# A fused attention and max-out kernel on one core: another head, column tiles for some output products, and a new order of the list

## The chip, the cores and the metric

The kernel runs on one core of a Trainium2 chip. The core has TensorE (matrix products; the profile shows its matmuls as PE and its weight loads as PEld), VectorE (DVE), ScalarE (ACT), GpSimd (POOL) and SyncE (SP), which run side by side and wait for one another by semaphores, and 16 DMA engines that serve queues issued here by SP and POOL. TensorE writes its results to PSUM, eight banks of 512 float32 columns in each of 128 partitions; DVE and ACT read them from there. The metric is the time of one execution on the device in microseconds, and its median over several runs. Less is better.

## The reference

Two attention steps through 32 inducing vectors, for each of four batches of 12544 rows of 128 channels, then a max-out layer over all 50176 rows:

```python
    scale = 1.0 / np.sqrt(C)
    I = np.broadcast_to(inducing[None], (B, m, C))

    def mab(q, kv):
        s = scale * (q @ kv.transpose(0, 2, 1))
        s = s - s.max(-1, keepdims=True)
        a = np.exp(s)
        a /= a.sum(-1, keepdims=True) + 1e-09
        return a @ kv
    h = mab(I, x)
    return mab(x, h).astype(np.float32)
...
    h1 = x @ w1
    h2 = x @ w2
    g = np.maximum(h1, h2)
    return (g @ w_out).astype(np.float32)
```

The sizes: x is 4 x 12544 x 128, inducing 32 x 128, w1 and w2 128 x 1024, w_out 1024 x 128, all float32.

## The kernel before

*What is computed.* The kernel first finds, for each batch, h (32 x 128), the pooled rows. It then never forms the second attention's output: it multiplies h by w2 - w1 ahead of time (`hwd`, 32 x 1024) and by w1 w_out (`m1`, 32 x 128), and uses max(a, b) = a + relu(b - a). For each chunk of 128 rows the exponentials of the scores against h (`e2`, 32 x 128) times `hwd` give the arguments of the ReLU (eight blocks of 128 x 128, laid with the hidden channel on the partitions); the ReLU's result times w_out is added up over the eight blocks in PSUM, and the product of `e2` and `m1`, called the linear part, is added to the same bank. At the end each row is scaled by the reciprocal of the sum of its 32 exponentials.

*The tiling.* A batch has 98 chunks. Four chunks, or runs of chunks, called quarters, form a block: the four quarters sit in the four groups of 32 partitions. TensorE is used in three modes. In full mode one product uses the whole array: the 3136 output products of line 932 (weights 128 x 128 from the ReLU's result, 128 columns of w_out), transposes, and the sums over the batch. In row mode the array is cut in four tiles of 32 rows, and four products of 512 columns run side by side, one for each quarter: `phase`, line 1085, both the ReLU's arguments (`e,hwd`) and the linear part (`m,e`). In column mode the array is cut in four tiles of 32 columns, again side by side: the scores of a block (`stage`, line 657), those of the pooling (`pool_scores`, line 356), and the pooling's sums (`pool_accum`, line 414).

*The stages.* The head (up to some 22 us) loads batch 0 in parts, transposes them on TensorE (`p1_transpose`, line 276; DVE copies one half of a part out of PSUM, ACT the other), takes their scores (line 292), exponentials (ACT, line 305), and adds up two sums in PSUM: line 319 (products with a column of ones, up to four chunks of 32 as weights) and line 328 (with x). All parts but the first are loaded by POOL's queue, which casts float32 to float16 on the way. w1 and w2 follow in halves, then w_out. Then come the sums' turn, the first 256 columns of `hwd`, the first block's scores (`stage_first`, line 684), and the main list. It works off the blocks of batch 0 and does the pooling of batch 1 between them, and so on; from batch 1 on x is transposed by DMA (line 208).

*What sets the order.* All engines but the DMAs run in the order in which the program is written. The main list is a string, `ORDER`, one word for each piece of work: a plain number is so many output products, `p4.13` a phase of four quarters (the second number's bits swap the engine chosen for a ReLU), `s` stages the next block, `x`, `c`, `t`, `a` are steps of the pooling, `g` turns the exponentials of a block for their sums (SP's transposing DMA, then POOL), `H`, `W` the late part of the weights (`H1` makes the second half of `hwd` and transposes the second half of w1; `W` multiplies w1 by w_out, line 607). `EVICT` says for each group of output products whether DVE or ACT scales it. While the program is built, the class `Clock` keeps an account of when each engine will be free; it decides which PSUM bank is taken (the one free first), whether ACT or DVE takes a ReLU (the one that would be done first), and whether filler products are put in (`keep_busy`, line 891). Nothing of it runs on the chip.

*Buffers.* Eight PSUM banks are eight tags of one pool; ReLU results have two buffers of 128 x 4096 float16 for each quarter; six output tiles wait for their stores, which SP issues.

## Time and profile before

| what | value |
|---|---|
| median of 3 runs | 318.21 us (317.64 to 318.43) |
| the profiled execution, its own time | 317.76 us |
| its span, first to last instruction | 316.0 us |
| granted clock of TensorE | 0.998 |
| TensorE's last product ends | 312.9 us after the span's start |
| busy shares: PE, ACT, DVE, POOL | 98%, 89%, 87%, 40% |
| HBM read and written | 27.28 MB, 25.69 MB |

The time of a run has about 1.8 us more in it than the span, which counts from the first instruction to the last. A busy share adds up the time in which at least one instruction of the engine is in flight; TensorE's products are pipelined (one of 128 columns is in flight for 219 ns, and the next starts after 56), so 98% doesn't say that nothing can be saved. Where an engine's idle time is given, the name behind the arrow is what ended it.

### The profile page before, as it was taken

The numbers are of one execution on the slowest core, as the hardware profiler recorded it, in microseconds if no ns is written. First come the engines' busy times: TensorE is split into PE (matmuls) and PEld (weight loads), VectorE is DVE, ScalarE is ACT, GpSimd is POOL, SyncE is SP. The second block draws the span as 40 slices with busy tenths as digits, with TensorE's granted clock in tenths as the row PEclk, the third lists the DMA queues.
The fourth block names the chain that finished last, engine by engine and source line by source line (L and its number), as shares of the span: only waits on it lengthen the run. The fifth ranks groups of instructions, "written<-read, shape, count | busy, mean of one in ns | idle before, by whom it ended". The sixth has DMA issues, their size and how long they took to land.

```text
span 316.0 us, 12577 instructions
## 1 busy us (share of the span) xinstructions
PE 308.6 (98%) x5308; PEld 239.9 (76%) x5308; DVE 274.5 (87%) x488; ACT 280.2 (89%) x580; POOL 125.8 (40%) x187
## 2 busy tenths in 40 slices
PE   6998999999999999999999999999999999999996
PEld 3885777777877777778877787887868777788885
DVE  2468999999878999988999899989899889999885
ACT  3669999999999999998999989899999999998891
POOL 7363060666620066067510064674406564461500
PEclk9999999999999999999999999999999999999999
DMA  8999999989799999898499999897323233324232
GB/s 203 208 252 205 207 219 146 207 229 230 127 218 245 245 183 174 190 233 207 121 225 252 213 227 215 204 174 203 106 85 118 100 106 118 119 88 140 102 120 101
DMA packets 81336, 55.81 MB, mean 177 GB/s; under 512 B 62816, under 2 KB 66176, under 8 KB 81280
## 3 DMA queue, kind: packets, MB, share of 16 engines
q1 hardware_dynamic: 75312, 41.32, 55.8%
q0 software_dynamic: 5968, 13.70, 22.4%
q8 instruction: 41, 0.67, 0.9%
q14 instruction: 15, 0.12, 0.1%
HBM read 27.28 MB, written 25.69 MB: 168 GB/s over the span
## 4 chain that ended last, share of the span: by engine, by line
PE 94%; DMA 2%; ACT 1%; DVE 1%; issue 1%; POOL 0%; POOLq 0%
PE ps L932 60%; PE ps L1085 23%; DMA xn<-in_x_dram 2%; PE ps L657 2%; PE ps L356 2%; PE ps L414 2%; PE ps L276 1%; PE ps L328 1%; PE ps L292 1%; PE ps L521 0%; DVE relu L1105 0%; PE ps L319 0%; ACT e L669 0%; DVE o L964 0%; ACT e_first L696 0%
## 5 line engine op out<-in xcount | busy, mean ns | idle before, releaser
L1102 ACT ACTIVATE relu<-ps 128x512 f16<-128x512 f32 x470 | 241.0, 627 | 17.5 <-PE ps L1085 16.5
L1105 DVE TENSOR_SCALAR relu<-ps 128x512 f16<-128x512 f32 x314 | 199.7, 684 | 20.6 <-PE ps L1085 19.0
L932 PE MATMUL ps<-woutp,relu 128*128 128x128 f16 x3136 | 203.5, 219 | 0.2
L932 PEld LDWEIGHTS <-relu 128*128 128x128 f16 x3136 | 176.6, 98 | 34.4 <-issue 28.7
L1085 PE MATMUL ps<-e,hwd 32*128 32x512 f16 (+2 forms) x840 | 82.8, 361 | 0.1
L720 POOL TENSOR_TENSOR half<-ed 128x256 f32<-128x256 f16 (+2 forms) x23 | 14.1, 613 | 145.8 <-DMA ed<-e 145.8
L724 POOL TENSOR_TENSOR rd<-den,minus 128x16 f32<-128x16 f32 (+2 forms) x23 | 60.7, 2639 | 1.8
L964 DVE TENSOR_TENSOR o<-ps,rd 128x512 f32<-128x512 f32 (+3 forms) x83 | 53.2, 643 | 3.9 <-PE ps L1085 2.8
L1085 PE MATMUL ps<-m,e 32*128 32x128 f16 x372 | 36.8, 216 | 0.0
L1085 PEld LDWEIGHTS <-hwd 32*128 32x128 f16 x880 | 26.7, 91 | 12.8 <-issue 3.8
L1085 PEld LDWEIGHTS <-e 32*128 32x128 f16 x372 | 22.4, 92 | 10.4 <-issue 2.7
L720 POOL TENSOR_TENSOR half<-half 128x32 f32<-128x32 f32 (+3 forms) x69 | 22.3, 323 | 5.4
L195 POOL DMA_DIRECT2D xn<-in_x_dram x32 | 17.6, 563 | 5.7 <-DMA xn<-in_x_dram 4.3
L280 DVE COPY xT<-ps 128x512 f16<-128x512 f16 (+3 forms) x12 | 5.7, 485 | 8.6 <-PE ps L276 8.6
L964 DVE TENSOR_TENSOR o<-ps,rp 128x512 f32<-128x512 f32 (+3 forms) x20 | 12.8, 642 | 0.0
L369 ACT ACTIVATE eu<-ps 128x512 f16<-128x512 f32 x18 | 11.0, 617 | 0.6 <-PE ps L356 0.3
L669 ACT ACTIVATE e<-ps 128x512 f16<-128x512 f32 (+2 forms) x21 | 11.1, 607 | 0.3 <-PE ps L657 0.2
L283 ACT COPY xT<-ps 128x768 f16<-128x768 f16 (+3 forms) x10 | 5.7, 574 | 4.3 <-PE ps L276 4.2
L276 PE MATMUL ps<-identity,xn 128*128 128x128 f16 x98 | 7.6, 220 | 1.4 <-DMA xn<-in_x_dram 0.9
L657 PE MATMUL ps<-xT,hT 128*32 128x512 f16 (+3 forms) x110 | 8.1, 361 | 0.1
L276 PEld LDWEIGHTS <-xn 128*128 128x128 f16 x98 | 5.5, 97 | 2.9 <-DMA xn<-in_x_dram 1.2
L356 PE MATMUL ps<-xT,inducingT 128*32 128x512 f16 x72 | 6.8, 386 | 0.0
(110 smaller groups left out, 117.7 us busy)
## 6 DMA issues: line engine op xcount, KB each, us to landing
out_dram<-o SPq DMA_DIRECT2D x90, 256.0 KB, 3.0
xn<-in_x_dram POOLq DMA_DIRECT2D x24, 448.0 KB, 10.4
out_dram<-o SPq DMA_DIRECT2D x10, 128.0 KB, 2.9
wf<-in_moe_w_dram POOLq DMA_DIRECT2D x4, 256.0 KB, 6.0
xn<-in_x_dram POOLq DMA_DIRECT2D x4, 224.0 KB, 10.2
xT<-xn SPq DMA_TRANSPOSE x33, 4.4
xf<-in_x_dram SPq DMA_DIRECT2D x1, 512.0 KB, 3.7
xf<-in_x_dram SPq DMA_DIRECT2D x1, 384.0 KB, 4.2
```

The lines of the kernel that those rows point to most:

```text
L195: nc.gpsimd.dma_start(out=xn_at[b, i][:, 0:n, :], in_=xr[b, :, k0 : k0 + n, :])
L276: nc.tensor.transpose(ps[:, j, :], xn[:, g + j, :], identity16)
L356: nc.tensor.matmul(out=ps[32 * g : 32 * (g + 1), :], lhsT=inducingT, rhs=xT_tiles[b % 2][:, U * u + 4 * g : U * u + 4 * (g + 1), :], start ...
L657: nc.tensor.matmul(out=ps[32 * q : 32 * (q + 1), 128 * t : 128 * (t + n)], lhsT=hq, rhs=xT[:, c : c + n, :], start=True, stop=True, tile_p ...
L669: nc.scalar.activation(out=blk.e2[:, 0 : 128 * wd], in_=ps[:, 0 : 128 * wd], func=AF.Exp, scale=st[0]["rs"] if blk.b == 0 else scale,)
L720: nc.gpsimd.tensor_tensor(out=dst, in0=cur[:, :, 0:n], in1=cur[:, :, n : 2 * n], op=ALU.add)
L724: nc.gpsimd.tensor_tensor(out=rp[:, 0:wd, :].rearrange("p t q -> p (t q)"), in0=den[:, 0 : 4 * wd], in1=minus1[:, 0 : 4 * wd], op=ALU.pow,)
L932: nc.tensor.matmul(out=g.ps[:, 128 * c : 128 * (c + 1)], lhsT=g.blk.relu[g.q][:, 128 * (jb * w4 + t) : 128 * (jb * w4 + t + 1)], rhs=woutp ...
L964: nc.vector.tensor_mul(osb[:, 0:m, :], g.ps[:, 0 : m * C].rearrange("p (s c) -> p s c", s=m), g.blk.rp[:, t0 : t0 + m, q : q + 1].broadcas ...
L1085: nc.tensor.matmul(**seq.pop(0))
L1102: nc.scalar.activation(out=dst, in_=src, func=AF.Relu)
L1105: nc.vector.tensor_scalar(out=dst, in0=src, scalar1=0.0, scalar2=None, op0=ALU.max)
```

## The change

The head: batch 0 is cut in 13 parts in place of 12 (the first from POOL's queue has 7 chunks). Parts 0 and 2 to 7 land as float32 in buffers that are free at that time (`homes`); DVE casts one half of a part, POOL the other (`cast_x`), and POOL's remaining loads are issued one by one between its casts (`load_next`), so each is behind the cast ahead of it. The sums with ones (line 319 before) take whole groups of four chunks: the exponentials stand in buffers padded with zeros, and the last two parts of two chunks are summed together. The order of the head's words is another, some copies out of PSUM change between DVE and ACT (`x` behind the word), and the sums over the identity go ahead of the first cast. The difference w2 - w1 is split in other pieces: DVE has one of 256 columns, POOL one of 256 and one of 512. POOL in place of ACT casts the second half of w1, before the last four loads of batch 1. The eight transposes of w1 go together, out of the head, into the list (`V`).

Output products in column tiles: a count with an `n` in the list puts each product as four, of 32 weight columns each, in the four column tiles. There are 44 such counts, 511 of the 3136 products, most of them beside `s`, `c` or `a`.

The list: all words of `ORDER`, the bits behind the phases, and `EVICT` are new. A third number of a phase holds ReLUs back: if the next unit of that quarter lands in the next bank, one instruction does both (1024 columns); `u` lets held ones go. 32 ReLUs become double. ACT evicts 38 pieces of 128 columns in place of 11.

The account (`Clock`): other constants, switching times by the mode that is left, a count of instructions fed to TensorE. Buffers: the eight banks are one tile, the ReLU buffers and output tiles are fixed in place of drawn from pools.

```diff
-    PAIR = 0.0558
-    SWITCH = {"full": 0.11, "row": 0.097, "col": 0.097}
+    PAIR = 0.0559
+    COLS = 0.0562
+    SWITCH = {
+        "full": {"row": 0.095, "col": 0.095},
+        "row": {"full": 0.082, "col": 0.088},
+        "col": {"full": 0.1, "row": 0.094},
+    }
+    STEP = 0.0035
+    FEED = 0.0133
+    AHEAD = 1.2
     LAT = 0.20
-    ROW = 0.224
...
-    def on_act(self, ready, us, tail=0.12):
+    def feed(self, n):
+        self.fed = max(self.fed, self.pe - self.AHEAD) + self.FEED * n
...
+    psall = psum.tile([128, 8, 512], F32, name="psall", tag="psall")
+    relus = [big.tile([128, 2, 4096], F16, name=f"relus{q}", tag=f"relus{q}") for q in range(4)]
+    relu1 = [big.tile([128, 1024], F16, name=f"relu1_{q}", tag=f"relu1_{q}") for q in range(2)]
...
-    parts[0] = [(0, 14), (14, 14), (28, 14), (42, 14), (56, 7), (63, 7), (70, 7), (77, 7), (84, 6), (90, 4), (94, 2), (96, 2)]
+    parts[0] = [(0, 14), (14, 7), (21, 7), (28, 14), (42, 14), (56, 7), (63, 7), (70, 7), (77, 7), (84, 6), (90, 4)]
+    parts[0] += [(94, 2), (96, 2)]
...
+        homes = {0: (2, 0, 0, 14), 2: (0, 1, 0, 7), 3: (1, 1, 0, 14), 4: (2, 1, 0, 14)}
+        homes.update({5: (0, 1, 7, 7), 6: (3, 1, 0, 7), 7: (3, 1, 7, 7)})
+        wide = {}
+        for i, (q, slot, k, n) in homes.items():
+            w = relus[q][:, slot, 256 * k : 256 * (k + n)].bitcast(F32)
+            wide[i] = w.rearrange("p (k c) -> p k c", c=C)
...
+        later = []
+        for i, (k0, n) in enumerate(parts[0]):
+            if i:
+                later.append((wide.get(i, xn_at[0, i]), xr[0, :, k0 : k0 + n, :]))
...
+        def load_next():
+            dst, src = later.pop(0)
+            nc.gpsimd.dma_start(out=dst, in_=src)
...
+        def cast_x(i):
+
+            for half, (g, m) in enumerate(cut(parts[0][i][1])):
+                eng = nc.gpsimd if half else nc.vector
+                eng.tensor_copy(out=xn_at[0, i][:, g : g + m, :], in_=wide[i][:, g : g + m, :])
+                done = ck.on_pool(LANDED[i], 0.1 + 0.19 * m) if half else ck.on_dve(LANDED[i], 0.05 + 0.083 * m)
+                st[0]["cast", i, half] = done
+            load_next()
...
+        pair16 = head16[:, 1024 : 1024 + 4 * M].rearrange("p (k m) -> p k m", m=M)
+        ets = {}
+        for ids, at, n in ((0, 3, 4), 1152, 14), ((1, 2, 5, 6), 2688, 7), ((9,), 3712, 6), ((10,), 3968, 4):
+            room = 4 * ((n + 3) // 4)
+            some = head16[:, at : at + len(ids) * room * M].rearrange("p (i k m) -> p i k m", i=len(ids), m=M)
+            if room > n:
+                nc.vector.memset(some[:, :, n:room, :], 0.0)
+            for j, i in enumerate(ids):
+                ets[i] = some[:, j]
...
+                if n > 2:
+                    cuts = [(et, j, 4) for j in range(0, n, 4)]
+                else:
+                    cuts = [(pair16, 0, 4)] if last else []
+                for src, j, m in cuts:
                     nc.tensor.matmul(
-                        out=st[0]["eps"][0 : m * M, 0:1],
-                        lhsT=et[:, j : j + m, :].rearrange("p k m -> p (k m)"),
...
-        1a 1b I S0 2a 2b S1 A0 S2 3a 3b A1 4a 4b S3 S4 A2 A3 5a 5b A4 6a 6b S5 7a 7b S6 A5 8a 8b S7
-        A6 9a 9b 10a S8 11a N S9 S10 A7 S11 A8 A9 A10 A11
+        1a 1b 0b C2 I 2b 2a S0 C3 S1 C4 S2 A0 A2 C5 3b A1 3ax 4a 4b S3 5b C6 5a 6a S4 C7 A3 S5 6b A4 L
+        7ax 7bx S6 A5 8bx 8a 9a 9b S7 A6 10bx 10a 11ax S9 12a N S8 S10 A7 S11 S12 A9 A8 A10 A11 A12
...
+        load_x(1, 0)
+        difference(nc.vector, 0, 256, 20.45, 0.34)
+        difference(nc.gpsimd, 256, 512, 20.45, 0.64)
+        load_x(1, 1)
+        load_x(1, 2)
+        difference(nc.gpsimd, 512, J, 22.35, 1.25)
+        cast_w1(1)
+        for i in range(3, 7):
             load_x(1, i)
...
+                nc.gpsimd.tensor_copy(out=w1h[:, sl], in_=w1f[:, sl])
+                w_of["cast"] = ck.on_pool(0.0, 0.8)
+
+        def weights_2():
+            turned = []
+            for g in range(2):
+                bi, ps = bank([128, 4, 128], F16)
+                for j in range(4):
+                    jb = 4 * g + j
+                    nc.tensor.transpose(ps[:, j, :], w1h[:, 128 * jb : 128 * (jb + 1)], identity16)
+                turned.append((bi, ps, ck.run(0.056 * 4, ready=max(ck.bank[bi], w_of["cast"] if g else 0.0), why="w")))
+                ck.bank[bi] = INF
+            for g, (bi, ps, end) in enumerate(turned):
+                if g == 0:
+                    nc.vector.tensor_copy(out=w1T[:, 0:4, :], in_=ps)
+                    ck.bank[bi] = w_of["w1T"] = ck.on_dve(end, 0.34)
+                else:
+                    nc.scalar.copy(out=w1T[:, 4:8, :], in_=ps)
...
+        def final_one(narrow=False):
...
+            tiles = [(32 * i, 32 * (i + 1)) for i in range(4)] if narrow else [(0, 128)]
+            for lo, hi in tiles:
+                nc.tensor.matmul(
+                    out=g.ps[lo:hi, 128 * c : 128 * (c + 1)],
+                    lhsT=relu[:, lo:hi],
+                    rhs=woutp[:, jb, :],
+                    start=not g.started,
+                    stop=(state["mm"] + 1 == n * NJB and g.linear),
+                    tile_position=(0, lo) if narrow else None,
+                    skip_group_check=True,
+                )
             g.started = True
-            end = ck.run(ck.PAIR)
+            ck.feed(8 if narrow else 2)
+            if narrow:
+                ck.wait(ck.fed, "feed")
...
+            on_act, on_dve = ((0.48, 0.6), (0.907, 1.133))[n - 1]
+            if (max(ck.act, ready) + on_act <= max(ck.dve, ready) + on_dve) != flip:
+                nc.scalar.activation(out=dst, in_=src, func=AF.Relu)
+                t = ck.on_act(ready, on_act)
+            else:
+                nc.vector.tensor_scalar(out=dst, in0=src, scalar1=0.0, scalar2=None, op0=ALU.max)
+                t = ck.on_dve(ready, on_dve)
+            for bi in banks:
...
+                near = [c for c, j in enumerate(free) if q in holds and c not in paired and j == holds[q][2] + 1]
+                if near:
+                    free[a], free[near[0]] = free[near[0]], free[a]
+                    paired.append(a)
...
+                if q in holds and k in paired:
+                    _, first, b0, _ = holds.pop(q)
+                    relu_out((q, blk), [first, unit], [b0, bi], ready, bool(flip >> k & 1))
+                elif q in holds:
+                    _, first, b0, ended = holds.pop(q)
+                    relu_out((q, blk), [first], [b0], ended, False)
+                    relu_out((q, blk), [unit], [bi], ready, bool(flip >> k & 1))
+                elif hold >> k & 1 and nxt and nxt[1:3] == unit[1:3] and nxt[3] == unit[3] + 1:
+                    holds[q] = (blk, unit, bi, ready)
+                    ck.bank[bi] = INF
+                else:
...
-        s p4.13 s H1 W g2 p4.1 p2 8 m0 4 p3 p2.1 10 p3 p2 13 p3.2 6 p4.5 22 p2 p4.8 17 x1.0 p4.8 4 g1 11
-        p4.1 13 p4.9 p1 16 p3.4 p2 14 p4.10 6 x1.1 4 x1.2 x1.3 x1.4 x1.5 x1.6 2 p3.6 s s s s 6 g3 6 p4.5
...
+        s p4.14.2 p1 s s s H1 V g2 4 p3.0.1 p2 W 2 p3.1 2 m0 9 p2.3.1 p3.1 x1.0 14 p2.2 p3 n17 x1.1 s
+        p4.9 x1.2 2 p2 n13 p4.3 n5 g3 n5 p4.6 11 g1 7 p4.4 10 p4.10 p1 n19 s p3.0.6 p2.1 12 p4.10 12 x1.3
+        4 x1.4 x1.5 4 x1.6 x1.7 x1.8 5 p3.6.3 p4.1 11 g4 13 p4.8 17 p4.0.12 p2.1 u 22 p3.2 8 p4.7 12 p1
+        c1.0 n5 p4.4 p1 n8 p2 5 p4 n2 g5 n11 p4.6 26 p4.7.13 p3.1 u n23 c1.1 p2.0.3 p3.1 8 t1.1 14 p4.2 6
...
-        EVICT = "000000000000000000000000101000000000000000000000010000000000000000000010000000000000000000000000000000010000"
+        EVICT = "100000000000000000001001001000000000000001000000011100010000000000000010000000000000000000000000000010100110"
 
...
-            "H": second_half,
+            "H": lambda v: small_hwd(0, (2,), bool(v)),
+            "V": weights_2,
             "W": weights_3,
             "f": linear_full,
+            "u": flush,
             "p": phase,
...
-            elif word.isdigit():
-                for _ in range(int(word)):
+            elif word.isdigit() or word[0] == "n":
+                narrow = word[0] == "n"
+                for _ in range(int(word.lstrip("n"))):
                     ready = final_ready()
-                    keep_busy(ready)
+                    if not narrow:
+                        keep_busy(ready)
                     ck.wait(ready, "relu")
-                    final_one()
```

286 lines of the change are left out of this document (142 added, 144 removed).

## The prediction

> **What bounds the kernel now.** I read the page's first parts, then the chain of waits, the groups by form, who waited for whom, and the timeline of TensorE, closely at the start and at one ordinary place.
>
> ```profile
> span 316.0 us, 12577 instructions
> PE 308.6 (98%) x5308; PEld 239.9 (76%) x5308; DVE 274.5 (87%) x488; ACT 280.2 (89%) x580; POOL 125.8 (40%) x187
> PE 94%; DMA 2%; ACT 1%; DVE 1%; issue 1%; POOL 0%; POOLq 0%
> L1102 ACT ACTIVATE relu<-ps 128x512 f16<-128x512 f32 x470 | 241.0, 627 | 17.5 <-PE ps L1085 16.5
> L1105 DVE TENSOR_SCALAR relu<-ps 128x512 f16<-128x512 f32 x314 | 199.7, 684 | 20.6 <-PE ps L1085 19.0 <-ACT relu L1102 0.6
> ```
> TensorE is the chain, 94% of it; ACT and DVE wait for it, not it for them. What is to be won is therefore in TensorE's own stream: in what it executes, in its changes of mode, and in the places where it stands still.
>
> ```profile
> 75.06 0.63 PE L414 MATMUL ps<-xn,eT 128*32 128x128 f16 x32
> 75.62 0.76 PE L1085 MATMUL ps<-e,hwd 32*128 32x512 f16 x7
> 76.31 1.23 PE L932 MATMUL ps<-woutp,relu 128*128 128x128 f16 x19
> 77.47 0.63 PE L414 MATMUL ps<-xn,eT 128*32 128x128 f16 x32
> 78.04 0.60 PE L1085 MATMUL ps<-e,hwd 32*128 32x512 f16 x5
> ...
> 78.58 1.79 PE L932 MATMUL ps<-woutp,relu 128*128 128x128 f16 x29
> ```
> First column start, second the time to the last end. Starts of single L932 products lie 55.9 ns apart: 19 make 1.06 us, and 77.47 - 76.31 is 1.16, so full to column costs 0.10. The 32 column products (8 per tile, four tiles side by side) last 8 x 55.9 = 0.45 of the 0.57 before the next row stretch: again 0.11 to 0.12 for the change and the first start. The row stretch at 78.04 is two rounds of 0.222 and 0.10. By such differences I take 0.105 from full to row (first start included), 0.093 back, 0.104 and 0.100 for full and column, 0.091 from column to row, 0.095 back.
>
> With these prices I laid the 5304 products of the instruction list end to end, from the first column products of the staging (22.22) on, each tile of the array one after the other: 251.9 us of work and 336 changes, 33.1 us, together 285.0. In the trace it is 22.22 to 312.93, 290.7. So 5.7 us are stalls: 1.7 before 28.3 us, some 4.0 over all the rest, in pieces of 0.03 to 0.43, nearly all inside row stretches, where a PSUM bank or a ReLU was late. The 1.7 are these:
>
> ```profile
> 22.22 0.40 PE L684 MATMUL ps<-xT,hT 128*32 128x256 f16 x8
> 23.44 0.41 PE L1085 MATMUL ps<-e_first,hwd 32*128 32x256 f16 x9
> 24.30 0.38 PE L521 MATMUL ps<-w,hT 128*128 128x512 f16 x1
> 24.73 0.39 PE L607 MATMUL ps<-woutp,w1s 128*128 128x128 f16 x4
> 26.09 0.40 PE L607 MATMUL ps<-woutp,w1s 128*128 128x128 f16 x4 [0.98 <-ACT w1s L599]
> 27.30 0.28 PE L891 MATMUL ps<-warm 128*128 128x128 f16 x2
> 27.70 0.40 PE L932 MATMUL ps<-woutp,relu 128*128 128x128 f16 x4
> ```
> L607 is the product of w1 and w_out; it stands 1.0 us for a copy on ACT, with all the rest behind it in order. The two L891 are fillers ahead of a late ReLU (0.3).
>
> **The change part by part, against the span of 316.0.**
>
> *Head, up to 22.22: -0.7.* Until 19.64 TensorE follows the landing of x. Six parts of x now land as float32 and are cast by DVE and POOL. In the trace a packet that casts (3584 bytes written, 7168 read) took 285 ns, an uncast one of 4096 bytes 159, that is 278 for 7168: 2.5% of the 9 us that these 56 columns take, -0.2; none at all is the one end, -0.5 (a 5% spacing) the other. The added casts are by L784's row (128x1024, 0.70 us) some 3 us of DVE, which sat idle 8.6 us there for transposes, and about half of each part on POOL; POOL's nearest row is the 128x512 subtraction, 1.27 us, so up to 1.9 us for 768 columns. The late parts, which set the end, are still cast by the transfer, so a slow POOL delays only earlier ones; uncovered it would cost up to 1 us. Then the tail of the chain. The sum products of L319 with 64 columns of weights started 93 to 124 ns from their neighbours, the others about 26:
>
> ```profile
> 21.02 0.19 PE L319 MATMUL ps<-ones,head 128*64 128x1 f16 x1
> 21.14 0.21 PE L328 MATMUL ps<-head,xn 128*128 128x32 f16 x2
> 21.28 0.19 PE L319 MATMUL ps<-ones,head 128*64 128x1 f16 x1
> 21.41 0.22 PE L328 MATMUL ps<-head,xn 128*128 128x32 f16 x2
> ```
> Padded to four chunks of zeros and joined to one at the end, they lose some 0.35 here; the transposes of w1 (L589) leave this place, and DVE does one difference fewer ahead of the reciprocal: -0.1 more. After that sum -0.65, rounded to -0.7; ends +0.5 and -1.2.
>
> *The start, 22.2 to 28.3: -1.2.* Three stagings (three times 0.22 and little switching) now stand before the second half of hwd, the transposes of w1 come later and both together, and two phases and four output products stand between them and L607's successor. So the 1.0 us at 26.09 and most of the 0.3 at 26.96 should be covered by work that was to be done anyway. Against it: the cast of w1's second half moves from ACT (0.62) to POOL behind a 1.27 us subtraction that ended at 24.24; at 0.6 to 1.3 it ends at 24.9 to 25.5, and the four transposes that wait for it have the finals queued behind them. That gives back 0.2 to 0.7. Four loads of the next batch are issued behind this cast, about 1 us later than at 24.19; three others are queued ahead of them at 2.2 us each, which hides it. I take 1.7 less 0.5; ends -1.9 and 0.
>
> *The laid-out list: +0.6.* The changed list laid by the same prices: 253.5 us of work and 328 changes, 32.1. Its row stretches have 257 rounds in place of 250 (92 of two, 61 of one and 4 of three in place of 97, 53 and 1): 7 x 0.222 = +1.5, some tiles being half filled. Eight changes fewer and dearer ones replaced by cheaper: -1.0. So the change does not shorten what TensorE is asked to do. This term has little spread.
>
> *511 of 3136 products in column tiles: +0.5.* Laid out, four products 128x32 side by side cost the 55.9 of one, but 8 instructions in place of 2: 7.0 ns each. The trace has that density only for the 32 to 38 products of L414, which showed no stretch; the runs are now up to 23 steps, 92 products. The lower end is 0. The upper: steps beyond 9.5 in a run, 175 in all by the list, are fed at the slowest rate of small products in the trace, L292's 25 ns (0.50 us for 14, 0.18 of it the last's own): 175 x (4 x 25 - 55.9) = 7.7. As L292 ran no faster after it had stood, its 25 ns look like the array's and not the feed's; I stay near L414 with 0.5.
> [...]
>
> *Stalls of the rest: -1.4.* 32 ReLUs are held and done two banks at a time. From seven ReLUs in 3.54 us on ACT one follows another by 0.485, on DVE (three in 1.89) by 0.60; at 0.83 and 1.04 ns an element (rows of 768 and 384, and of 512 and 128 columns) a double one saves 0.05 to 0.07, 2 us over both engines; but 27 more evictions of 128 columns on ACT (0.25 to 0.38 each) and 14 more ReLUs on DVE eat that: DVE +4, ACT -1 to +2. Neither is relieved; a held bank also is gone for a phase. What can gain is the new order alone. The space between a unit's last product and the next use of its bank or ReLU, in laid-out time, is below 1.3 us for 74 of 752 ReLUs in place of 86 of 784: a little looser. Of 4.0 I let a third go; ends -3.5 and +2.
>
> Sum: -0.7 - 1.2 + 0.6 + 0.5 - 1.4 = -2.2, a span of 313.8. The profiled run took 317.8, 1.8 more than its span, and the median of the runs, 318.2, another 0.4 more: 313.8 + 2.2 = 316.0 us.
>
> **Rivals.** *The feed decides* (slower): runs of column steps come at a rate between L414's and L292's. For it: 8 instructions a step, 44 runs where there was none, no row of that length. Against: L414. At half the bound, 3.9 in place of 0.5, the span is 317.2, the time 319.4. From 2.7 us on, 15 ns for each of the 175 steps, nothing of the gain is left. Chance 0.2.
> *The stalls only move* (no change): the cast on POOL and DVE's longer queue put the start's stall at the transposes of w1 (-0.5 in place of -1.2), the held banks keep the 4.0. Sum -0.7 - 0.5 + 0.6 + 0.5 + 0 = -0.1: 318.1. For it: loads not relieved, spaces hardly looser. Against: the 1.0 at L607 has a clear cause, and it is taken out. Chance 0.17.
> *All stalls go*: -0.9 - 1.7 + 0.6 + 0 - 3.2 = -5.2, 313.0. For it: they are short and single; against: the same spaces. Chance 0.13. The forecast keeps 0.5.
>
> **How the numbers follow.** A measurement of this kernel tells 0.3%, 0.95 us, from no change: faster is below 317.3. Forecast and "all go" are faster but for 0.03; half of "only move" lies within, the rest to both sides: faster 0.64, within 0.17, slower 0.19. The range leaves out half of "all go" and a part of the feed's: 313.2 to 319.4; the likeliest's own is 314.5 to 317.3.
>
> **What would show it.** The first staging at 21.5 rather than 22.22; no wait of 1 us at the successor of L607; TensorE's end at about 311; in runs of column steps over ten a step of 56 ns (right) or of 70 to 100 toward the run's end (the feed); 157 row stretches of 0.33 or 0.55 with fewer beyond 0.6. Wrong it is if the start is as late as before, or column runs stretch, or waits of ReLUs for banks grow.

## The result and the profile after

The changed kernel takes 330.46 us (median of 4 runs, 329.82 to 333.36) beside 318.32 for the kernel before on the same chip: 1.040 times as long, 95% interval 1.034 to 1.047. It is slower, and outside the range of the forecast. The profiled execution has a span of 329.0 us; these lines are from its page:

```profile
span 329.0 us, 15652 instructions
PE 313.6 (95%) x6838; PEld 241.9 (74%) x6838; DVE 280.6 (85%) x487; ACT 281.2 (85%) x577; POOL 132.8 (40%) x196
...
PEclk9999799999999979999999999999999999999999
DMA  8999999996589999996479999969623435342432
...
q8 instruction: 53, 0.87, 1.1%
...
PE 90%; DMA 3%; issue 3%; DVE 1%; POOL 1%; ACT 0%; POOLq 0%
L1117 ACT ACTIVATE relus<-psall 128x512 f16<-128x512 f32 (+1 forms) x432 | 232.1, 631 | 30.0 <-PE psall L1194 28.6
```
TensorE has 5 us more of busy time, but 13 more of span: it stands idle for longer. ACT now waits 28.6 us for it (before 16.5), so ACT isn't what is late. "issue", time in which the profile shows nothing that an engine waits for, went from 1% to 3% of the chain. The clock has two dents. And queue 8, which carries instructions, brought 53 packets. The kernel before had:

```profile
PEclk9999999999999999999999999999999999999999
DMA  8999999989799999898499999897323233324232
...
q8 instruction: 41, 0.67, 0.9%
```
The list of who waited for whom, after and then before (total, times, longest, all us), tells in its last column that this is not more of the old short waits but a few long ones, without a releaser. I call such a long wait a stop; a stall is any idle time of TensorE beyond its list laid end to end.

```profile
PEld L996 <- issue: 35.4, 115, 2.4
```
```profile
PEld L932 <- issue: 28.7, 105, 0.8
```
The timeline of TensorE shows the first of them, in the middle of a run of column tiles, with no buffer or bank to wait for:

```profile
34.88 0.37 PE L1194 MATMUL psall<-e_first,hwd 32*128 32x512 f16 x1
35.18 0.23 PE L996 MATMUL psall<-woutp,relus 128*32 128x128 f16 x2
37.66 1.14 PE L996 MATMUL psall<-woutp,relus 128*32 128x128 f16 x38 [2.25 <-issue]
38.73 0.61 PE L1194 MATMUL psall<-e,hwd 32*128 32x512 f16 x4
39.28 0.93 PE L996 MATMUL psall<-woutp,relus 128*128 128x128 f16 x7
```
Numbering all of TensorE's records in order of time (weight loads and matmuls, two for a product, and the ten records of its sequencer), every long stop stands at the same place of a period of 256. "Packet" is that of queue 8 which arrives at the stop; all of them have 16384 bytes, that is 64 for each of 256 records:

```
stop (us)        length  record mod 256   packet starts  ends     from its end to the next product
35.18 -  37.66    2.47       193             35.23       36.15      1.51
43.46 -  44.40    0.94       193             41.91       43.09      1.32
109.20 - 109.94   0.74       193            107.58      108.47      1.47
113.05 - 114.76   1.72       193            112.55      113.48      1.28
142.41 - 143.04   0.63       193            140.66      141.55      1.49
146.41 - 148.02   1.61       193            145.65      146.54      1.48
177.11 - 178.78   1.67       193            176.37      177.35      1.43
```
The period is that of the packets: 13686 records make 53.5 times 256, and 53 packets came (before 10626, 41.5 and 41). I call 256 instructions a page, and count a page from one record 193 to the next, so that a stop stands where a page is used up; why the place is 193, no run shows. With three shorter ones the stops are 10.0 us. All lie before 180 us, where the DMA engines are busy (a share of 0.96 from 23 to 180 us); after 212 us their share is 0.47 and no stop is over 0.1. After two stops the granted clock fell to 0.50, for some 3.4 us each time (37.8 to 41.2 us and 116.3 to 119.7); in the last line of the timeline above seven full products take 0.93 in place of 0.56. If TensorE could have worked all that time, half speed took another 3.4 us in all; this is an upper value. Here are the windows 23 to 60, 100 to 120 and the end, after and then before (length; busy time of PE, PEld, DVE, ACT, POOL; granted clock, DMA share, GB/s):

```profile
23.00:60.00 37.00, 33.38 (x733) 23.34 (x733) 30.96 (x54) 31.28 (x64) 14.07 (x19) 0.95 1.15 186
100.00:120.00 20.00, 18.03 (x443) 13.75 (x440) 16.14 (x27) 15.64 (x34) 4.31 (x6) 0.91 1.11 227
...
212.00:326.00 114.00, 113.86 (x2283) 92.10 (x2277) 102.94 (x170) 102.07 (x206) 48.54 (x66) 1.00 0.47 123
```
```profile
23.00:60.00 37.00, 35.72 (x559) 26.15 (x559) 34.89 (x62) 35.42 (x73) 12.25 (x17) 1.00 1.09 191
100.00:120.00 20.00, 20.00 (x328) 15.19 (x328) 18.68 (x32) 18.99 (x40) 5.04 (x7) 1.00 1.02 219
```

**The page theory (P).** The packet of the next page starts at the earliest about when a page is entered (in the changed kernel 0.4 us ahead of it to 4.25 behind). How long it waits goes with the other traffic: in the kernel before 1.0 us in the median until 180 us, with a DMA share of 0.9 to 1.1, and 0.2 after 205, with 0.4. It takes some 1.0 us, and 1.3 to 1.5 later, at a stop, the first instruction of its page runs. From entering a page to the next page's use that makes, as an estimate from these parts, 2.5 us where the packet hardly waits, and 6.7 with the longest wait seen. The kernel before uses a page up in 7.8 us (median before 180 us, 5.3 the shortest) and is never late by more than 0.1, though its longest wait of a packet was 4.17. The changed kernel uses one in 5.1 (3.0 the shortest; the stops themselves taken off), as a product in column tiles has eight instructions in place of two. The rivals tested against it: F, the forecast's own slow case, each small instruction or each column step costs some ns more wherever it stands; and L, the new list, head and buffers are what costs. A fourth, data that land late, has the list of waits of the changed kernel against it: from 24 us on TensorE waited for a transfer of data once, 0.4 us (L470 for `eT`; before 0.2), and ACT and DVE never.

### The profile page after: what moved, and what is told of

It is laid out like the page before. It is cut to its first block, busy times and chain, and to the rows that moved or that the text cites. A ratio compares the mean times of both kernels' runs of the same rounds, so it can differ in the third digit from the quotient of the medians.

```text
span 329.0 us, 15652 instructions
## 1 busy us (share of the span) xinstructions
PE 313.6 (95%) x6838; PEld 241.9 (74%) x6838; DVE 280.6 (85%) x487; ACT 281.2 (85%) x577; POOL 132.8 (40%) x196
## 4 chain that ended last, share of the span: by engine, by line
PE 90%; DMA 3%; issue 3%; DVE 1%; POOL 1%; ACT 0%; POOLq 0%
PE psall L996 59%; PE psall L1194 23%; DMA relus<-in_x_dram 3%; PE psall L710 2%; PE psall L470 2%; PE psall L411 1%; POOL relus L280 1%; DVE relus L1120 1%; PE psall L318 1%; PE psall L578 1%; PE psall L383 0%; PE psall L334 0%; PE psall L516 0%; DVE hwd L582 0%; PE psall L660 0%
## 5 line engine op out<-in xcount | busy, mean ns | idle before, releaser
L1117 ACT ACTIVATE relus<-psall 128x512 f16<-128x512 f32 (+1 forms) x432 | 232.1, 631 | 30.0 <-PE psall L1194 28.6
L1120 DVE TENSOR_SCALAR relus<-psall 128x512 f16<-128x512 f32 (+1 forms) x312 | 206.0, 710 | 25.7 <-PE psall L1194 23.6
L996 PE MATMUL psall<-woutp,relus 128*128 128x128 f16 (+1 forms) x4613 | 206.9, 222 | 4.8 <-issue 4.8
L996 PEld LDWEIGHTS <-relus 128*128 128x128 f16 (+1 forms) x4613 | 178.0, 98 | 40.4 <-issue 34.7
L1194 PE MATMUL psall<-e,hwd 32*128 32x512 f16 (+2 forms) x840 | 85.1, 363 | 0.0
L1031 DVE TENSOR_TENSOR osbs<-psall,rd 128x512 f32<-128x512 f32 (+1 forms) x76 | 49.3, 650 | 5.3 <-issue 2.2
L1194 PE MATMUL psall<-m,e 32*128 32x128 f16 x372 | 37.4, 216 | 1.4 <-issue 1.4
L774 POOL TENSOR_TENSOR half<-half 128x32 f32<-128x32 f32 (+3 forms) x69 | 22.3, 324 | 5.4
L1031 DVE TENSOR_TENSOR osbs<-psall,rp 128x512 f32<-128x512 f32 (+2 forms) x18 | 11.9, 661 | 1.0 <-PE psall L1194 0.5
L723 ACT ACTIVATE e<-psall 128x512 f16<-128x512 f32 (+2 forms) x21 | 11.3, 570 | 0.7 <-PE psall L710 0.7
L425 ACT ACTIVATE eu<-psall 128x512 f16<-128x512 f32 x18 | 10.9, 612 | 0.5 <-PE psall L411 0.4
```

The costliest lines, as they stand in the source:

```text
L425: nc.scalar.activation(out=eu, in_=ps, func=AF.Exp, scale=scale, accum_out=st[b]["es"][:, u : u + 1])
L723: nc.scalar.activation(out=blk.e2[:, 0 : 128 * wd], in_=ps[:, 0 : 128 * wd], func=AF.Exp, scale=st[0]["rs"] if blk.b == 0 else scale,)
L774: nc.gpsimd.tensor_tensor(out=dst, in0=cur[:, :, 0:n], in1=cur[:, :, n : 2 * n], op=ALU.add)
L996: nc.tensor.matmul(out=g.ps[lo:hi, 128 * c : 128 * (c + 1)], lhsT=relu[:, lo:hi], rhs=woutp[:, jb, :], start=not g.started, stop=(state["m ...
L1031: nc.vector.tensor_mul(osb[:, 0:m, :], g.ps[:, 0 : m * C].rearrange("p (s c) -> p s c", s=m), g.blk.rp[:, t0 : t0 + m, q : q + 1].broadcas ...
L1117: nc.scalar.activation(out=dst, in_=src, func=AF.Relu)
```

## The experiments

Ratios are against the kernel before on the same chip, with 95% intervals; "stops" sums what is lost at the period's place.

**E1, no column tiles.** The changed kernel with all counts plain.
```diff
-                narrow = word[0] == "n"
+                narrow = False
```


> The changed kernel with every output product in full mode (an n in the list is read as a plain count). Laid end to end its list is 289.6 us from the first staging on (353 changes of mode), against 285.6 with columns and 285.0 before: +3.9 on the changed kernel. Theory P (pages: TensorE's instructions come in pages of 256 over the same DMA engines, two are at hand, and a page used up sooner than the next lands stops the engine): with 10.6 thousand instructions again, all stops of 0.5 us and more at the 193rd of 256 go, some 12 us: span 329.0 + 3.9 - 12 = 321, time about 323. Theory F (feed: each column step costs 12.2 us / 511 = 24 ns for its eight instructions, wherever it stands): the same time. Theory S (the new order, the held ReLUs and the head cost it): it stays at 329 + 4 = 333.

329.51 us, 1.036 (1.034 to 1.037), span 327.9. The long stops are gone (0.6 us left) and the clock is 1.0, as P says. But the time hardly fell: laid end to end this list is 289.6 us, 4.0 more than with column tiles (the changes of mode come back), and some 12 us of stalls are left, two thirds of them in row stretches. The 323 that P (and F) expected was missed. Taking the column tiles out of an order that was made with them makes another order; the run shows the cause of the stops, not what the list is worth.

**E2, column tiles late.** Plain counts up to the 1900th product, then every second count in column tiles (608 products, where the DMA engines are less busy).
```diff
+        words = 0
...
-                narrow = word[0] == "n"
+                words = words + 1
+                narrow = state["done"] >= 1900 and words % 2 == 0
```


> As the kernel without columns, but from the 1900th output product on (after 212 us, where the DMA engines are less than half busy) every second count is put in column tiles: 608 steps, more than the changed kernel's 511, all late. Laid end to end +2.1 us against no columns. Theory P: pages come in time there (waits of 0.1 to 0.6 us for a packet, used up in 3 us or more), so no stops: no columns + 2 us. Theory F: 608 x 24 ns = 14.6 more, no columns + 17 us.

340.18 us, 1.071 (1.068 to 1.074): 10.7 over E1, between what P and F had expected. The stops are 8.8 us, all beyond 228 us and the long ones all at record 193, with a DMA share of 0.31 there. The 2.1 us that this list is longer than E1's and the 8.2 more of stops are 10.3 of the 10.7, so nothing much is left for a price of each column step (F). P's place was right and its price wrong: at the seven long stops a page was used up in 2.0 to 3.3 us, while its successor took 3.6 to 4.0 from entry to use, as packets still waited 1.0 to 1.7. DMA engines as busy as in the first 180 us are not needed.

**E3, more instructions without column tiles.** The kernel before, with each row product of more than 128 columns cut into products of 128: the same work, the same order, 0.4 us more laid end to end, 15138 records in place of 10626.
```diff
-                        out=ps[:, 128 * w * jj : 128 * w * (jj + 1)],
+                        out=ps[:, 128 * (w * jj + t) : 128 * (w * jj + t + 1)],
...
-                        rhs=blk.e2[r, 128 * t0 : 128 * (t0 + w)],
+                        rhs=blk.e2[r, 128 * (t0 + t) : 128 * (t0 + t + 1)],
...
-                    for jj in range(jpb)
+                    for jj in range(jpb) for t in range(w)
```


> The kernel before, its row products of 512 and 256 columns cut in products of 128: 15.1 thousand instructions in place of 10.6 on TensorE, no column tile added, laid end to end +0.4 us. Theory P: pages are used up in 5.4 us on average in place of 7.7, while a packet waits up to 4.2 us, takes 1.0 and 1.3 more till its first use; so stops appear at the page ends, in the first 220 us alone, a few of 0.5 to 2 us: time 320 to 326. A theory that column tiles themselves cost (their weight loads, their bank): 318 to 319, no stops.

327.81 us, 1.031 (1.028 to 1.035), more than the 320 to 326 expected. The old list, head and buffers get stops as well, 7.1 us, the long ones at record 193 and before 185 us. Its timeline:

```profile
182.51 0.41 PE L1085 MATMUL ps<-e,hwd 32*128 32x128 f16 x15
184.76 0.23 PE L1085 MATMUL ps<-e,hwd 32*128 32x128 f16 x1 [1.84 <-issue]
```
Fifteen of sixteen products of one stretch run, and the last waits 1.84 us for nothing. So such stops come with the number of instructions; they need neither column tiles nor the new list.

**E9, the same cut, but late.** As E3, from the 1900th product on (1590 records more).
```diff
+                step = 1 if state["done"] >= 1900 else w
...
-                    for jj in range(jpb)
+                    for jj in range(jpb) for t in range(0, w, step)
```


> The kernel before with its row products cut in products of 128 columns only from the 1900th output product on (after some 205 us, where the DMA engines are less than half busy): 1590 instructions more on TensorE, all late. Theory P: a page is used up in 5 us there, a packet waits 0.1 to 1.9 us, takes 1.0 and 1.3 more: no stops, time as before, 318 to 319. If each further instruction cost, as the 9.7 us for 4510 of the split rows everywhere would make it: +3.4, 321.5.

318.86 us, 1.003 (1.002 to 1.004), span 316.7. In spite of pages of 5.2 us (median; 4.5 the shortest) there is no stop, packets waiting 0.4 there in the median:

```profile
276.34 0.40 PE L1086 MATMUL ps<-e,hwd 32*128 32x128 f16 x16
276.67 0.90 PE L932 MATMUL ps<-woutp,relu 128*128 128x128 f16 x13
277.50 0.40 PE L1086 MATMUL ps<-e,hwd 32*128 32x128 f16 x16
```
Sixteen small products start and end within 0.40 us, and the next stretch follows at 0.33. A price for each instruction of the size that F needs (3.4 us here) is refuted: the time rose by 0.8 us. The same instructions cost most where a page is late: 9.7 us for 4512 more records in E3, 0.8 for 1590 here.

**E4, less DMA.** The changed kernel without the loads of batches 2 and 3 and without the stores of the first 64 groups.
```diff
-        nc.gpsimd.dma_start(out=xn_at[b, i][:, 0:n, :], in_=xr[b, :, k0 : k0 + n, :])
+        if b < 2:
+            nc.gpsimd.dma_start(out=xn_at[b, i][:, 0:n, :], in_=xr[b, :, k0 : k0 + n, :])
...
+                if g.index >= 64:
```


> The changed kernel, its TensorE stream untouched, without the loads of batches 2 and 3 (old rows are taken in their place) and without the stores of the first 64 groups of output products: the DMA engines are less busy between 60 and 212 us. Theory P: the stops at 109, 113, 118, 142, 146 and 177 us (0.5 to 1.7 each, about 7 with the lowered clock behind them) shrink or go, those at 35 to 45 stay: span about 322. Theory F: 329 as before.

325.07 us, 1.023 (1.019 to 1.026): 5.4 less than the changed kernel, and the stops are 4.7 in place of 10.0. Those at 109, 113, 146 and 177 are gone, and the one at 142 stays (0.59); those at 35 (2.64) and 44 (0.94) stay too, where batch 1 is still loaded. Where the changed kernel stood 1.72 us inside a row stretch, now:

```profile
112.66 0.22 PE L1196 MATMUL psall<-m,e 32*128 32x128 f16 x1
112.66 0.40 PE L1196 MATMUL psall<-e,hwd 32*128 32x512 f16 x3
112.73 0.33 PE L1196 MATMUL psall<-m,e 32*128 32x128 f16 x3
112.89 0.38 PE L1196 MATMUL psall<-e,hwd 32*128 32x512 f16 x2
```

**E5, the stream shifted by half a page.** 68 products of eight columns in place of four fillers at the start: 128 records more.
```diff
-    WARM = 9
+    WARM = 5
...
+        for _ in range(68):
+            nc.tensor.matmul(out=ps[:, 0:8], lhsT=warm[:, 0:128], rhs=warm[:, 0:8], start=True, stop=True)
```


> The changed kernel with 68 products of 8 columns in place of four of the nine warming ones of 512, early in the head: the rest of TensorE's stream is the same, 128 instructions further on. Theory P: the stops sit again at the 193rd instruction of 256, counted from the program's start, so at other places of the list, half a page earlier in it. If a stop belongs to a place of the list (a bank, a late ReLU, a long run of column steps), it stays at that place, and its count moves by 128, to the 65th. The time may go either way by some us.

333.85 us, one execution. The longest stops (39.38, 2.49 us; 107.05, 1.67; 174.65, 3.07) are again at record 193, that is at other products of the list. Shorter ones near 135, 141 and 148 us (up to 1.5) stand at 209, 223 and 144; they are all inside stretches of L411, and for the last two the profile names another cause, x not yet transposed by DMA:

```profile
149.26 0.40 PE L411 MATMUL psall<-xT,inducingT 128*32 128x512 f16 x3 [1.10 <-DMA xT<-xn]
```
The seven products at which the changed kernel had its long stops pass without one.

**E6, the old list under the new head.** The changed kernel with `ORDER` and `EVICT` of the kernel before (`H1 W` as `H1 V W`), no column tiles.
```diff
-        s p4.14.2 p1 s s s H1 V g2 4 p3.0.1 p2 W 2 p3.1 2 m0 9 p2.3.1 p3.1 x1.0 14 p2.2 p3 n17 x1.1 s
...
+        s p4.13 s H1 V W g2 p4.1 p2 8 m0 4 p3 p2.1 10 p3 p2 13 p3.2 6 p4.5 22 p2 p4.8 17 x1.0 p4.8 4 g1 11
...
```


> The changed kernel's head, account and buffers with the list and the evictions of before (the transposes of w1 right behind H1), no column products: 10.6 thousand instructions. Laid out 287.4 from the first staging, +2.4 on before, since other banks and phases are picked. The head of the changed kernel reaches its first staging at 22.30 as before (22.22). Theory P: no stops at page ends; the time is before's plus the 2.4 and its late ReLUs: 320 to 323. If the head or the fixed buffers had cost the 12 us, it is at 328 or more.

324.09 us, 1.019 (1.017 to 1.021), a little over the 320 to 323 expected; span 323.0, 287.4 laid end to end, with no long stop of the page's kind (0.5 us in all). So head, account and buffers bring no gain with that list either. Of its some 9.5 us of stalls 1.5 are one wait for `W`'s operand on DVE (25.98 to 27.46), where the kernel before stood 1.2 us, and up to 1.7 are a clock of 0.50 from 27.8 to 31.2.

**E8, the start alone.** The kernel before with three stagings ahead of `H1` and `W` behind two phases.
```diff
-        s p4.13 s H1 W g2 p4.1 p2 8 m0 4 p3 p2.1 10 p3 p2 13 p3.2 6 p4.5 22 p2 p4.8 17 x1.0 p4.8 4 g1 11
-        p4.1 13 p4.9 p1 16 p3.4 p2 14 p4.10 6 x1.1 4 x1.2 x1.3 x1.4 x1.5 x1.6 2 p3.6 s s s s 6 g3 6 p4.5
+        s p4.13 s s s s H1 g2 p4.1 p2 W 8 m0 4 p3 p2.1 10 p3 p2 13 p3.2 6 p4.5 22 p2 p4.8 17 x1.0 p4.8 4 g1 11
+        p4.1 13 p4.9 p1 16 p3.4 p2 14 p4.10 6 x1.1 4 x1.2 x1.3 x1.4 x1.5 x1.6 2 p3.6 s 6 g3 6 p4.5
```


> The kernel before with three words moved: the stagings of blocks 2 to 4 ahead of H1 in place of their place behind the transposes of batch 1, and W after two phases. The start of the changed kernel alone. The stops of 1.0 and 0.3 us between 24.3 and 28.3 go: if the prediction's step was right, 0.8 to 1.3 us faster than before (317); if they only move, no change.

319.11 us, 1.005 (1.003 to 1.006): not faster. The wait of 1 us at L607 is gone (0.18 are left), but 20 to 40 us hold 4.8 us of stalls in place of 1.9: products wait for exponentials on ACT (0.20 and 0.18 us), which has those of the added blocks to make, and for the second half of `hwd` (0.4). But in the profile the clock was 0.50 from 28 to 34.5 us, which may be up to 3.4 of the 4.8. The six executions without such a dip have spans of 317.05 in the median, before 316.2: 0.8 us are lost at full clock too, and no profile shows where.

**E7, the double ReLUs undone.** The changed kernel, each ReLU of 1024 columns as two of 512 on the same engine.
```diff
-                nc.scalar.activation(out=dst, in_=src, func=AF.Relu)
+                for d, s in both:
+                    nc.scalar.activation(out=d, in_=s, func=AF.Relu)
...
-                nc.vector.tensor_scalar(out=dst, in0=src, scalar1=0.0, scalar2=None, op0=ALU.max)
+                for d, s in both:
+                    nc.vector.tensor_scalar(out=d, in0=s, scalar1=0.0, scalar2=None, op0=ALU.max)
```


> The changed kernel with each of the 32 double ReLUs (1024 columns) done as two of 512 on the same engine, one behind the other; TensorE's stream is the same, laid end to end 285.6 as before. Page theory (TensorE stops where its next page of 256 instructions has not come): the stops stay at their places, 330.5 +- 1. Rival, the held banks with their double ReLUs are what takes the gain: the first of two results then is there some 0.5 us sooner and its bank free sooner, the stalls in row stretches shrink by 2 us or more, below 328.5. Other way: a double ReLU saves 0.05 to 0.07 of engine time each, 2 us over both engines; if ACT and DVE are what is late, two singles cost up to +1.

331.56 us, 1.045 (1.042 to 1.048), not told apart from the changed kernel; the span is 329.0 again, with 11.0 us of stops, the long ones at the same records. Held banks are not where the time went.

**E10, a few column tiles.** The kernel before, short counts beside `s`, `c` or `a` after the 1200th product in column tiles: 96 products. (In the changed kernel 21 of the 44 column counts stand beside one of these words, so not most of them.)
```diff
+                beside = [v for v in list_[max(at - 1, 0) : at + 2] if v[0] in "sca"]
+                narrow = state["done"] >= 1200 and int(word) <= 16 and len(beside) > 0
...
-                    final_one()
+                    final_one(narrow)
```


> The kernel before, with only those counts of output products in column tiles that stand beside s, c or a, have at most 16 products and come after the 1200th product: 96 products, 285 more matmuls, five changes of mode fewer, laid end to end 284.5 in place of 285.0. Page theory: the runs are short and single, so a page lasts longer than the 3.5 us that fetching one takes there, no stop: -0.5, 0.998 of the kernel before. Rival, column tiles cost something by themselves (each step over 56 ns, or the switch): at 15 ns a step +1.4, at the forecast's upper bound of 44 ns a step +4, 1.004 to 1.013.

319.27 us, 1.005 (1.003 to 1.007), span 317.1. It was to be slightly faster; it is slower by just one stop, at record 193:

```profile
166.28 0.51 PE L935 MATMUL ps<-woutp,relu 128*128 128x128 f16 x6
167.68 1.01 PE L935 MATMUL ps<-woutp,relu 128*128 128x128 f16 x15 [0.89 <-issue]
```
It stands among plain products. The page that ended here was used up in 4.5 us, part of it being column products; the packet of the next waited 3.29 us, took 0.96 and was used 1.30 after its end, 5.55 in all, so 1.05 were missing. In the kernel before the page of that stretch lasted 7.8. The 0.5 us of saved changes do not show in the time.

**E11 and E12, both kernels without most DMA, zeros in its place.** No loads of batches 1 to 3, no stores of the first 64 groups; DVE writes zeros to the buffers of batch 1.
```diff
+        if b == 0:
...
+        for i in range(7, 12):
+            nc.vector.memset(xn_tiles[i], 0.0)
...
+                if g.index >= 64:
```


> The changed kernel without the loads of batches 1 to 3 (their buffers hold zeros or older data) and without the stores of the first 64 groups of output products; TensorE's stream is untouched, 285.6 us laid end to end. It asks what the list is worth when no page of instructions is late. Page theory: with little else in the DMA engines a page takes 0.2 us of wait, 1.0 of transfer and 1.35 until its first use, 2.5 us, and the changed kernel never uses one up in under 3.0: no stop over 0.3 us, the clock stays at 1.0, the span loses the 10.0 us of stops and the 3.4 of halved clock, 329.0 - 13.4 = 315.6, +- 1.5, and it is within 1.5 us of the kernel before without the same transfers. Rival, the list is poor by itself (the runs with it and no stops, plain counts or the old list under the new head, were 11 and 6 us over the kernel before): ReLUs and banks stay late, and it keeps 4 us or more over the kernel before without the same transfers. Rival, column tiles cost more than 56 ns a step: the same 4 us or more, but in column runs.

> The kernel before without the same transfers, as the measure for the changed kernel without them. It has no stop for a page to lose, so both theories expect 316.0 less what its transfers delay, 0 to 1.5 us: 0.995 to 1.0 of the kernel before.

321.15 us (1.009, 1.007 to 1.011) and 319.81 (1.005, 1.003 to 1.006): 1.3 us apart. The zeros delayed the main list of E12 by 3 us in the profile, against its expectation, and the profiled execution of E11 took 619 us, its output products 344 ns each in place of 220, so its stops can't be read. The next pair leaves out the zeros.

**E13 and E14, the same without zeros.** Batches 1 to 3 read batch 0's rows where they lie.
```diff
-            xn_at[b, i] = xn_tiles[(7 * b + k0 // P1) % NXN][:, off : off + n, :]
+            xn_at[b, i] = xn_tiles[k0 // P1][:, off : off + n, :]
...
+        if b == 0:
...
+                if g.index >= 64:
```


> The changed kernel without the loads of batches 1 to 3 (they read batch 0's rows where these lie) and without the stores of the first 64 groups; nothing is put in their place, and TensorE's stream is untouched, 285.6 us laid end to end. Page theory: no page is late, the span loses the 10.0 us of stops and the 3.4 of halved clock: 315.6, +- 1.5, within 1.5 us of the kernel before without the same transfers. Rival, the list is poor by itself: it keeps 4 us or more over that kernel. The run with zeros in place of the loads points to the first: 1.3 us over its partner, though its profile was of no use and its head was late by its own zeros.

> The kernel before without the same transfers, the measure for the changed kernel without them: 316.0 less 0 to 1.5 us by both theories, 0.995 to 1.0 of the kernel before.

320.18 us (1.008, 1.005 to 1.011) and 317.71 (0.999, 0.998 to 1.000). Without these transfers the distance of the two kernels falls from 12 us to 2.5, so some ten of the twelve hang on the DMA traffic, though no line of the change issues a transfer in the main list. The windows of E13 beside those above:

```profile
100.00:120.00 20.00, 20.00 (x539) 15.16 (x539) 19.01 (x32) 18.45 (x39) 9.13 (x12) 1.00 0.85 121
...
140.00:180.00 40.00, 39.30 (x864) 30.70 (x850) 37.32 (x65) 35.62 (x75) 12.60 (x21) 1.00 0.41 62
```
P expected no stop over 0.3 us and a distance within 1.5: neither is met in full, as five stops of together 1.8 us are left in the main list (0.89 the longest, at 140.9: page used up in 3.4 us, packet waiting 1.8). A poor list, 4 us or more, is further off. And all six executions of E13 have a mean clock of 0.989 to 0.995, where E14's ten have 1.0: at 0.995 some 1.6 us of clock are missing, which may be part of the 2.5. In the profile the clock was 0.50 from 22.9 to 29.7 us; that execution was the longest of the six (322.94), so its span isn't compared.

## Why the prediction was wrong

Sum of the forecast and of the profile, by the same terms (first staging, laid list, stalls, end):

| step | forecast | measured | how |
|---|---|---|---|
| head | -0.7 | +0.1 | first staging at 22.30, before 22.22 |
| start | -1.2 | -0.4 | stalls of 20 to 30 us: 1.25, before 1.7 |
| laid-out list | +0.6 | +0.6 | 285.6 of 325.9 - 22.3; the other 18.0 are stalls |
| column products (feed) | +0.5 | +13.4 | stops 10.0, halved clock 3.4 (upper value) |
| stalls of the rest | -1.4 | -0.7 | 18.0 - 13.4 - 1.25 = 3.3, before 4.0 |
| sum | -2.2 | +13.0 | 329.0 - 316.0 |

*The step that failed* is "511 of 3136 products in column tiles: +0.5", with ends 0 and 7.7. I asked how fast single small products can start, took L414's runs as proof that 14 ns an instruction is possible, and that was right: where no page is late a run of columns goes at its price, here 76 records of 19 products to the next start in 1.08 us, 56.8 ns a step:

```profile
227.85 1.25 PE L996 MATMUL psall<-woutp,relus 128*32 128x128 f16 x76
228.93 0.61 PE L411 MATMUL psall<-xT,inducingT 128*32 128x512 f16 x8
```
What I left out is that instructions have to be brought. Neither end of the range held it, as both came from rates within a run, and the supply works over pages of 256 (packets of 16384 bytes, all long stops of the changed kernel at record 193). The profile of the kernel before had the row for it, "q8 instruction: 41", with the DMA share near 1 in a line above; 2 x (4 x 511 - 511) = 3066 instructions more are twelve pages more (41 and 53), and they fall where the list has them dense. The packet of the next page starts 0.4 us ahead of a page's entry at the earliest (0.5 in the kernel before), so no trace here shows more than two pages at hand, the one in use and the next. In the kernel before that was enough (pages of 7.8 us in the median, none late by more than 0.1); with pages used up in 3.0 to 5.8 us, as at the long stops, it wasn't (0.6 to 2.5 us each).

*The rival "the feed decides"* had the sign and the place, and a chance of 0.2, but its mechanism, small products that start late one by one, is refuted (E9), and its 319.4 was 11 us short.

*Head.* The last part of x landed at 19.53 (before 19.64), but its transposes start at 19.92 (before 19.69), and the last exponentials end at 21.22 (before 20.84): loads without the cast are not what sets the end. Behind these exponentials the last sum starts after 0.12 us (before 0.57), so the joined sums won what was forecast, and the later exponentials took it back. Then w2's first half landed at 21.38 (before 20.96), as its load is now issued behind casts on POOL, so DVE did the difference late and `hT` behind it; after and then before:

```profile
21.40 0.42 DVE L625 TENSOR_TENSOR w<-relus 128x256 f16<-128x256 f32 x1 [0.47 <-DMA relus<-in_moe_w_dram]
21.75 0.28 DVE L530 TENSOR_SCALAR hT<-psall 128x128 f16<-128x128 f32 x1
```
```profile
20.98 0.43 DVE L573 TENSOR_TENSOR w<-wf 128x256 f16<-128x256 f32 x1 [0.23 <-DMA wf<-in_moe_w_dram]
21.66 0.29 DVE L473 TENSOR_SCALAR hT<-ps 128x128 f16<-128x128 f32 x1 [0.25 <-PE ps L328]
```
The +0.1 is one profile's: in five others with this head (E1, E2, E4, E6, E7) the first staging is at 21.9 to 23.1, in five with the old one (E3, E8, E9, E10, E14) at 22.15 to 22.54. So this head is hardly faster, and rather slower.

*Start.* L607's successor (now L660) waits no longer, as forecast. The forecast had a give-back of 0.5 at the transposes of w1, behind POOL's cast; these (L643) run without a long wait, and TensorE waits for the second half of `hwd` on DVE:

```profile
25.04 0.73 PE L643 MATMUL psall<-identity,relus 128*128 128x128 f16 x8
...
26.56 0.78 PE L1194 MATMUL psall<-e_first,hwd 32*128 32x128 f16 x12 [0.37 <-DVE hwd L582]
27.27 0.62 PE L660 MATMUL psall<-woutp,relus 128*128 128x128 f16 x8
```
E8 has the order alone: the same wait removed, the time is 1.1 us longer (1.005 of the kernel before). My reading is that this stall is a lack of finished operands, and that work moved in front needs operands of its own, which ACT and DVE have to make first; no run shows it by itself.

*The list* came out as laid. Its looser order can't be read in the changed kernel, where every stop lets ACT and DVE catch up; after 180 us, without stops, its stalls are 1.7 us and before 1.1. Of the 2.5 us that E13 is behind E14, 1.8 are stops in the profiled execution, and a dip of the clock may be another 1.6. So without late pages the change would be about even with the kernel before, not the 2.7 us ahead that the sum gives without its feed term; this is worked out from runs that leave transfers out, and no run shows the full computation so.

*Open:* how much of the 3.4 us the halved clock cost; what the column tiles would be worth in an order made without late pages (E1 and E6 changed the list along with them); why a page is first used 1.3 to 1.5 us after its packet ends; why packets waited over 1 us in E2 with a DMA share of 0.31. No version beat the kernel before.

## What to carry to other kernels

Cutting a product into tiles costs instructions even where it costs no array time (here eight in place of two, at 56.8 ns a step beside 55.9): count instructions per microsecond over windows of 256, and compare the time in which the list uses up such a page with what a page takes to come (here an estimated 2.5 us where the packet hardly waits, 3.6 to 4.0 at the stops of E2, up to 6.7 with the longest wait of a packet, 4.25, at a DMA share of 1.13). Dense stretches late in the list had no stop with pages of 4.5 us or more and packets that waited 0.4 in the median (E9), and 8.8 us of stops with pages of 2.0 to 3.3 and waits of 1.0 to 1.7 at the long stops (E2). So, if a late page is possible, I would put the dense stretches where packets wait little, and far apart; no run here has such an order. In a profile like these, long waits for "issue" without a releaser, at a fixed place of 256 records (here 0.6 to 2.5 us at record 193), point to this; a stop at a plain product may come from dense code in the page that ends there (E10: used up in 4.5 us, 7.8 in the kernel before).

## What was not expected of the hardware

Two stops of 2.5 and 1.7 us were followed by some 3.4 us at a granted clock of 0.50, so a stop may cost more than its length (up to 1.7 us more each here, if the lower clock is its doing); 1.7 us at 177 was not (1.00 in 177 to 184 us), nor were 2.5 and 2.2 us in E7 (1.00 behind both). One instruction packet of 16 KB waited 4.25 us from the entry into a page, while the DMA engines moved some 195 GB/s; the packets of the changed kernel took 0.9 to 1.7 us themselves.
